# A linear-attention and mixture-of-experts kernel: a query's feature maps meet the state in two row tiles of 64 features by 128 tokens, where they met in four quarters of 64 by 64

## The chip, the cores and the metric

The kernel runs on one core of a Trainium2 chip. The metric is the device time in microseconds (us) of one execution; the median of a few runs is given, and one further execution is taken by the profiler. Nearly everything is computed in 32-bit floats; many operands are split into a high and a low part, so that three matmuls of reduced precision (fp32r) stand for one exact product. The matmuls that the change touches are plain fp32 ones.

## The reference

Two mixers of the same 2048 tokens of 448 features are weighted by a gate per token. A is linear attention with 16 heads of 28 features and a learned feature map, B a mixture of 8 experts of which each token uses two.

```python
q, k, v = heads(x @ wqkv)                                   # 16 heads, Dh = 28
phi = lambda p: concat([softmax(p @ w_phi), softmax(-(p @ w_phi))])   # 56 features a head
kv  = einsum("bhsf,bhsd->bhfd", phi(k), v)                  # the state, summed over tokens
z   = einsum("bhsf->bhf", phi(k))
num = einsum("bhqf,bhfd->bhqd", phi(q), kv)
den = einsum("bhqf,bhf->bhq", phi(q), z) + 1e-6
a   = (num / den) @ wo
b   = sum over the token's two experts e of gate_e * (silu(x @ w1[e]) @ w2[e])
g   = sigmoid(sum(x * gate_w))
out = g * a + (1 - g) * b
```

The change is in `num` and `den`: the maps of the queries times the state.

## The kernel before

The kernel has three stages on the time axis. Up to about 113 us it makes the keys' maps and sums the state over 16 row tiles of 128 tokens (`key`, `norm`, `state`, and `value` for the values), and folds weights together (`fold`, line 308, whose small fp32 matmuls `wf` are the same kind of quarters as those of the change). From 113 to about 204 us the queries' maps meet the state, again one row tile of 128 tokens after the other. After that the experts run, two matmul layers each (`hp` at lines 139 and 1038, `acc` at lines 1122, 1138 and 1156), to the end at 791 us.

In the middle stage, the pass of the loop for row tile t puts these on TensorE, in this order:

- `attend(t)` (line 909), the block `n`: exponentials of the query tile, turned so that features are on partitions (`et`), against the block-diagonal state `B`. A head has 64 partitions: 56 features and a pad of zeros. `et[t]` has eight columns of blocks (`NJ = 8`), and in each the partitions 0 to 63 are one head and 64 to 127 another, so all 16 heads are covered. `B` holds 28 + 28 + 4 = 60 columns for a head: the state for the positive and for the negative softmax, and the sums for the denominators.
- `flip(t + 2)` (line 729), the block `et`: 16 transposes that turn the maps of a later tile, in two row tiles of the array (64 rows by 128 columns each).
- `turn(t - 1)` (line 948), the block `ot`: eight transposes of the previous tile's result, in the same two row tiles.
- `project(t - 2)` (line 139), the block `ao`: eleven matmuls of 128 by 128 with the output weights.
- `ask(t + 7)` (line 658), the block `pq`: eleven matmuls of 128 by 128 that make the query projection of a later tile; in the later passes its place is taken by transposes of tokens for the first expert (`xgt`).

VectorE then reads `n` in `weigh` (reciprocals `r` and `n`, products `z` and `w`, lines 919 to 925), and GpSimd sums the two signs (`om`). There is one PSUM tile for `n`, two banks wide (`two_banks`, tag "T", one buffer), so `n` of the next row tile waits until VectorE has read this one. The first index of its view, `a`, picks the bank and the half of the partitions of `et`; `b` picks the half of the tokens.

The order on TensorE, ACT and VectorE is the order of the program in this part (a manual schedule). SyncE issues transfers in an order that the scheduler chooses from modelled times; its queue holds the stores of finished rows (`aos`, line 960), the loads of small tables (`byrank`, `tabm`, `tabx`) and the loads of the experts' weights (`wr`, line 772).

A shape such as 64*64 in the profile is the part of the array that an instruction uses, rows by columns. A plain fp32 matmul is two records, one for each pass, and each has a weight load of its own (LDWEIGHTS, on the row PEld), whose columns are the stationary operand's: here the tokens.

Of the kernel before, what the change touches and what calls it, by code (L numbers as in the profile page):

```python
# [84 lines left out]
def gated_mix(ctx: ExitStack, tc: tile.TileContext, xt, xq, wk, wq, wv, wphi, wo, w12, out):  # L85
    nc = tc.nc
# [18 lines left out]
    def two_banks(name, tag="T"):  # L105
        pool, n = banks[tag]
        return pool.tile([P, NJ, P], F32, tag=tag, name=name, bufs=n)
# [26 lines left out]
    reached = {}  # L134
# [77 lines left out]
    start = ExitStack()  # L212
# [28 lines left out]
    for what in LANDING:  # L241
        t = int(what[1])
# [57 lines left out]
    half = [slice(64 * a, 64 * a + 64) for a in range(2)]  # L300
# [65 lines left out]
    for what in LANDING:  # L366
        t = int(what[1])
# [297 lines left out]
    B = px.tile([P, NJ, 60], F32, name="B")  # L665
    nc.gpsimd.tensor_copy(B[:, :, 58:60], hsign.unsqueeze(1).to_broadcast([P, NJ, 2]))

    def blocks(kvs):
        nc.scalar.activation(kvs[:, :, 0:56], kvp[:, 0:224].rearrange("p (g f) -> p g f", g=4), AF.Copy)
        yield  # L670
        kvt = bank("O", "kvt")
        for g in range(0, 4, 2):
            nc.tensor.transpose(kvt[:, g * 64:g * 64 + P], kvs[:, g:g + 2].rearrange("p g f -> p (g f)"), ident)
        kv = kvt[:, 0:256].rearrange("p (j d) -> p j d", j=NJ)[:, :, 0:DH + 1]
        nc.scalar.activation(B[:, :, 0:DH + 1], kv, AF.Copy, scale=hsign[:, 0:1])
        nc.vector.tensor_scalar(B[:, :, DH + 1:58], kv, hsign[:, 1:2], None, op0=ALU.mult)
# [43 lines left out]
    et = {}  # L720
# [33 lines left out]
    b = blocks(kvs)  # L754
# [149 lines left out]
    def attend(t):  # L904
        n_ = two_banks(f"n{t}").rearrange("p (a j) (b d) -> p a (j b) d", a=2, b=2)
        for j in range(NJ):
            for a, h in enumerate(half):
                for b in half:
                    reached["n"] = nc.tensor.matmul(n_[b, a, j, 0:60], et[t][h, j, b], B[h, j], start=True, stop=True)  # L909
        return n_.rearrange("p a j d -> p (a j) d")  # L910

    def weigh(t, n_):
# [301 lines left out]
    for t in range(NT + 2):  # L1214
# [15 lines left out]
        if t < NT:  # L1230
            n_ = attend(t)
# [76 lines left out]
    for s in range(E * NFC):  # L1308
# [15 lines left out]
        if e < LARGE:  # L1324
# [5 lines left out]
            while len(held) > (1 if e == 0 or fc == 0 else 2):  # L1330
                h = held.pop(0)
# [5 lines left out]
        n = 3 * nm  # L1337
        if e == E - 1 and fc > NFC - LATE:
            n = n // 2 if fc < NFC - 1 else 0
# [121 lines left out]
```

## Time and profile before

| | |
|---|---|
| median of 3 runs | 787.98 us (787.19 to 788.23) |
| the profiled execution, its own time | 793.1 us |
| its span, first to last instruction | 791.1 us |
| mean granted TensorE clock | 0.993 |
| TensorE busy (PE), weight loads (PEld) | 776.4 us, 717.7 us |
| VectorE, ScalarE, GpSimd busy | 481.0, 308.6, 335.3 us |
| block n, line 909 | 1024 records of a load, 1024 of a matmul, 113.6 to 199.6 us |

Matmuls are pipelined: a record of a matmul lasts from its issue to a modelled end, and records overlap, so the sum of busy time says less than the distance from the start of one block to that of the next. Weight loads overlap matmuls. "issue" as a releaser means that the engine waited for nothing that the profile shows. Times in the profile count from the start of the span.

### The profile page before, as it was taken

The numbers are of one execution on the slowest core, as the hardware profiler recorded it, in microseconds if no ns is written. First come the engines' busy times: TensorE is split into PE (matmuls) and PEld (weight loads), VectorE is DVE, ScalarE is ACT, GpSimd is POOL, SyncE is SP. The second block draws the span as 40 slices with busy tenths as digits, with TensorE's granted clock in tenths as the row PEclk, the third lists the DMA queues.
The fourth block names the chain that finished last, engine by engine and source line by source line (L and its number), as shares of the span: only waits on it lengthen the run. The fifth ranks groups of instructions, "written<-read, shape, count | busy, mean of one in ns | idle before, by whom it ended". The sixth has DMA issues, their size and how long they took to land.

```text
span 791.1 us, 18474 instructions
## 1 busy us (share of the span) xinstructions
PE 776.4 (98%) x7542; PEld 717.7 (91%) x7542; DVE 481.0 (61%) x1044; ACT 308.6 (39%) x523; POOL 335.3 (42%) x318
## 2 busy tenths in 40 slices
PE   8999999999999999999999998999999999999995
PEld 6888878888999999998998898999999999999994
DVE  4698977768776865665574443554744555475431
ACT  5543455556532443343342322332433333243221
POOL 5667877885123235414540445144325405523003
PEclk9999999999999999999999998999999999999998
DMA  8320000153333346326541552363445436434403
GB/s 274 125 86 1 2 2 26 27 119 138 121 140 127 105 90 180 99 81 148 157 131 53 116 149 91 107 153 128 123 119 151 135 118 161 137 129 109 138 2 47
DMA packets 39788, 85.95 MB, mean 109 GB/s; under 512 B 11312, under 2 KB 20928, under 8 KB 39700
## 3 DMA queue, kind: packets, MB, share of 16 engines
q1 hardware_dynamic: 29332, 67.88, 25.9%
q0 software_dynamic: 10224, 16.61, 11.3%
q8 instruction: 61, 1.00, 0.6%
q10 hardware_dynamic: 144, 0.23, 0.1%
q14 instruction: 27, 0.22, 0.1%
HBM read 71.89 MB, written 12.82 MB: 107 GB/s over the span
## 4 chain that ended last, share of the span: by engine, by line
PE 86%; issue 9%; DVE 1%; POOL 1%; ACT 1%; DMA 0%; SPq 0%; POOLq 0%; DVEq 0%; ACTq 0%
PE hp L1038 17%; PE acc L1122 17%; PE hp L139 15%; PE acc L1156 13%; PE ao L139 5%; PE pk L139 5%; PE pq L658 3%; PE pv L139 3%; PE n L909 2%; PE pv L353 1%; PE early L658 1%; PE kv L637 1%; PE et L729 1%; POOL out_dram L994 1%; PE acc L1138 1%
## 5 line engine op out<-in xcount | busy, mean ns | idle before, releaser
L1122 PE MATMUL acc<-w2h,hx 64*128 64x448 f32 (+3 forms) x1088 | 193.5, 365 | 0.1
L1071 ACT ACTIVATE hs<-hp 128x272 f32<-128x272 f32 (+4 forms) x154 | 70.8, 484 | 312.2 <-issue 190.0
L828 POOL DMA_INDIRECT xg<-in_xq_dram,idq x114 | 125.5, 1101 | 156.6 <-PE hp L1038 56.5
L1077 DVE CAST hx<-hs 128x504 fp32r<-128x504 f32 (+5 forms) x154 | 55.4, 360 | 209.9 <-ACT hs L1071 203.9
L1122 PEld LDWEIGHTS acc<-w2h,hx 64*128 64x128 f32 (+3 forms) x1088 | 159.6, 184 | 5.9 <-ACT y L1179 1.5
L1122 PE MATMUL acc<-w2l,hx 64*128 64x448 f32 (+3 forms) x544 | 153.8, 365 | 0.0
L1038 PE MATMUL hp<-xgl,w1h 64*128 64x504 f32 (+2 forms) x490 | 144.6, 386 | 1.9 <-issue 1.9
L1038 PE MATMUL hp<-xgh,w1h 64*128 64x504 f32 (+2 forms) x490 | 145.0, 386 | 0.6 <-issue 0.6
L1038 PE MATMUL hp<-xgh,w1l 64*128 64x504 f32 (+2 forms) x490 | 144.4, 387 | 0.1
L994 POOL DMA_INDIRECT out_dram<-y,tabm x32 | 52.2, 1632 | 172.4 <-DVE y L1181 164.0
L1156 PE MATMUL acc<-w2h,hx 128*128 128x448 f32 (+2 forms) x366 | 111.7, 365 | 0.0
L1122 PEld LDWEIGHTS acc<-w2l,hx 64*128 64x128 f32 (+3 forms) x544 | 95.7, 184 | 1.6
L1038 PEld LDWEIGHTS hp<-xgl,w1h 64*128 64x128 f32 x490 | 86.2, 185 | 4.6 <-issue 1.8
L1038 PEld LDWEIGHTS hp<-xgh,w1h 64*128 64x128 f32 x490 | 86.3, 185 | 4.2 <-issue 1.3
L1038 PEld LDWEIGHTS hp<-xgh,w1l 64*128 64x128 f32 x490 | 85.9, 185 | 4.0 <-issue 0.9
L1080 DVE TENSOR_TENSOR hx<-hs,hx 128x276 fp32r<-128x276 f32 (+5 forms) x168 | 84.9, 512 | 5.3
L139 PE MATMUL hp<-xgh,w1h 128*128 128x272 f32 (+1 forms) x336 | 87.9, 289 | 0.0
L139 PE MATMUL hp<-xgh,w1l 128*128 128x272 f32 (+1 forms) x336 | 87.8, 289 | 0.0
L797 DVE TENSOR_TENSOR w1l<-wr,w1h 128x1024 fp32r<-128x1024 f32 x56 | 68.2, 1218 | 10.9 <-ACT w1h L795 10.0
L1156 PEld LDWEIGHTS acc<-w2h,hx 128*128 128x128 f32 (+2 forms) x366 | 68.0, 186 | 6.2 <-issue 0.7
L1156 PE MATMUL acc<-w2l,hx 128*128 128x448 f32 (+2 forms) x190 | 69.4, 365 | 0.0
L139 PEld LDWEIGHTS hp<-xgh,w1l 128*128 128x128 f32 x336 | 63.2, 188 | 0.6
(235 smaller groups left out, 1396.1 us busy)
## 6 DMA issues: line engine op xcount, KB each, us to landing
wr<-in_w_dram SPq DMA_DIRECT2D x56, 512.0 KB
wr<-in_w_dram SPq DMA_DIRECT2D x46, 448.0 KB
kept<-in_w_dram SPq DMA_DIRECT2D x10, 448.0 KB
out_dram<-aos SPq DMA_DIRECT2D x16, 224.0 KB
xr<-in_xt_dram SPq DMA_DIRECT2D x10, 256.0 KB
xg<-in_xq_dram,idq POOLq DMA_INDIRECT x114
xr<-in_xt_dram SPq DMA_DIRECT2D x6, 192.0 KB
out_dram<-zero SPq DMA_DIRECT2D x5, 224.0 KB
```

The lines of the kernel that those rows point to most:

```text
L139: reached["pe"] = nc.tensor.matmul(o, a, b, start=i == 0, stop=i == n - 1)
L658: nc.tensor.matmul(pq[t].rearrange("p h d -> p (h d)"), x, w, start=k == 0, stop=k == 10)
L797: nc.vector.tensor_tensor(out=l, in0=raws[s][layer - 1], in1=h.bitcast(F32), op=ALU.subtract)
L828: i = nc.gpsimd.indirect_dma_start(out=t[:, b], out_offset=None, in_=xq, in_offset=bass.IndirectOffsetOnAxis(ap=idq[:, e, 4 * c + b:4 * c ...
L909: reached["n"] = nc.tensor.matmul(n_[b, a, j, 0:60], et[t][h, j, b], B[h, j], start=True, stop=True)
L994: return nc.gpsimd.indirect_dma_start(out=out, out_offset=bass.IndirectOffsetOnAxis(ap=idx_ap, axis=0), in_=y, in_offset=None, compute_op= ...
L1038: meet(("first", i), a, lambda: nc.tensor.matmul(o[i], l, r, start=n == 0, stop=n == len(rounds) - 1), n == 0)
L1071: nc.scalar.activation(hs[:, tsl], hp, AF.Silu)
L1077: nc.vector.tensor_copy(h[:, tsl], hs[:, tsl])
L1080: nc.vector.tensor_tensor(out=h[:, a + o:b + o], in0=hs[:, a:b], in1=h[:, a:b].bitcast(F32), op=ALU.subtract)
L1122: meet((e, c), a, lambda: nc.tensor.matmul(acc[e][c][:l.shape[1], 0:D], l[half[a]], r[half[a]], start=new, stop=ends and c not in of[k + 1 ...
L1156: i = nc.tensor.matmul(acc[e][c][:l.shape[1], 0:D], l, r, start=fc == 0 and k == 0, stop=fc == NFC - 1 and k == len(pr) - 1)
```

## The change

The loop over the two halves of the tokens goes; the stationary operand is now all 128 tokens of the tile (64 rows by 128 columns) instead of 64 of them (64 by 64), and the result covers all 128 partitions of its bank instead of half of them. The moving operand stays the 60 columns of `B`. So a row tile has 16 matmuls instead of 32, on two row tiles of the array instead of four quarters. What is computed is the same, and lands in the same places.

```diff
         n_ = two_banks(f"n{t}").rearrange("p (a j) (b d) -> p a (j b) d", a=2, b=2)
         for j in range(NJ):
             for a, h in enumerate(half):
-                for b in half:
-                    reached["n"] = nc.tensor.matmul(n_[b, a, j, 0:60], et[t][h, j, b], B[h, j], start=True, stop=True)
+                reached["n"] = nc.tensor.matmul(n_[:, a, j, 0:60], et[t][h, j], B[h, j], start=True, stop=True)
         return n_.rearrange("p a j d -> p (a j) d")
```

On TensorE's queue, in the pass for the third row tile, the rows before (a name, its number, then the partitions and columns that are written):

```order
L658 MATMUL pq_1827<-WHq,XL_178 128x448 x3
L909 MATMUL n_1854<-B,et_1693 64x60 [waits DVE_49,PE_49]
L909 MATMUL n_1854<-B,et_1693 64x60 x31
L729 MATMUL et_1903<-ident,eq_210 128x64 [waits Activation_49,Pool_49]
L729 MATMUL et_1904<-ident,eq_210 128x64 [waits Activation_49]
```

and now:

```order
L658 MATMUL pq_1795<-WHq,XL_178 128x448 x3
L908 MATMUL n_1822<-B,et_1677 128x60 [waits DVE_49,PE_49]
L908 MATMUL n_1822<-B,et_1677 128x60 x15
L729 MATMUL et_1855<-ident,eq_210 128x64 [waits Activation_49,Pool_49]
L729 MATMUL et_1856<-ident,eq_210 128x64 [waits Activation_49]
```

Nothing moved on TensorE: 32 rows became 16, of twice the partitions, with the same waits, between the same neighbours. The queues of VectorE, ScalarE and GpSimd hold the same instructions in the same order.

On SyncE's queue, at the end of the small tables and the start of the experts' weights, the rows before:

```order
L971 DMA tabm<-tabd 128x4x2
L960 DMA out_dram<-aos_2632 128x448
L772 ISA
L772 DMA wr_0_2777<-in_w_dram 128x1024
L772 ISA
L772 DMA wr_0_2778<-in_w_dram 128x896
```

and now:

```order
L970 DMA tabm<-tabd 128x4x2
L772 ISA
L772 DMA wr_0_2633<-in_w_dram 128x1024
L959 DMA out_dram<-aos_2504 128x448
L772 ISA
L772 DMA wr_0_2634<-in_w_dram 128x896
```

The sixth store of a finished row moved behind the first load of weights. The fourth and the fifth moved in the same way, behind five and one more loads of `byrank`; the other stores stand where they stood.

## The prediction

> **What bounds the kernel now.** I read the page first (busy shares, then the chain that ended last), then the chain in order of time around the changed line, then the busy time by stage, and last the weight loads kept apart by shape.
>
> ```profile
> PE 776.4 (98%) x7542; PEld 717.7 (91%) x7542; DVE 481.0 (61%) x1044; ACT 308.6 (39%) x523; POOL 335.3 (42%) x318
> PE 86%; issue 9%; DVE 1%; POOL 1%; ACT 1%; DMA 0%; SPq 0%; POOLq 0%; DVEq 0%; ACTq 0%
> 113.60:204.00 90.40, 89.00 (x1650) 78.88 (x1650) 68.87 (x167) 55.02 (x98) 63.15 (x59) 1.00 0.26 73
> 204.00:791.00 587.00, 576.17 (x4662) 544.45 (x4660) 324.56 (x695) 198.97 (x314) 194.64 (x157) 0.99 0.42 119
> ```
>
> TensorE is busy 98% of the span and makes up 86% of the chain. The two rows by stretch give its busy time first, then weight loads, DVE, ACT, POOL, the granted clock and the DMA share. In the stage of the change (113.6 to 204 us) it works 89.00 of 90.40 us at full clock, so what is put on it or taken from it there moves the end, but for 1.4 us. After 204 us it is again the engine that everything waits for. The chain in one ordinary row tile of this stage (start, length, what):
>
> ```profile
> 137.06 1.09 PE n L909 x64
> 138.15 0.64 PE et L729 x16
> 138.79 0.25 PE ot L948 x8
> 139.04 2.43 PE ao L139 x11
> 141.47 2.22 PE pq L658 x11
> 143.70 1.09 PE n L909 x64
> ```
>
> Nothing but TensorE stands between one tile's n and the next, 6.64 us later: no wait of 0.1 us is in it. The changed block is 1.09 us of it. It has 64 records for 32 matmuls: fp32 goes in two passes, each with its own weight load.
>
> **What sets those 1.09 us.** The change makes half as many matmuls of twice the width, so all depends on whether a pass costs its issue, its streaming, or its weight load. First the same block as loads (PEld) and matmuls (PE), with two blocks of other code for comparison (start, length from first to last, count):
>
> ```profile
> 143.62 1.02 PEld L909 LDWEIGHTS n<-B,et 64*64 64x64 f32 x64 [0.30 <-issue]
> 144.71 0.57 PEld L729 LDWEIGHTS et<-ident,eq 64*128 64x128 f32 x16
> 145.21 0.33 PEld L948 LDWEIGHTS ot<-ident,om 64*128 64x128 f32 x8
> 143.63 1.16 PE L909 MATMUL n<-B,et 64*64 64x60 f32 x64
> 19.60 1.97 PEld L308 LDWEIGHTS wfk<-bd,wraw_k 64*64 64x64 f32 x128 [0.31 <-issue]
> 48.32 0.45 PEld L637 LDWEIGHTS kv<-ek,v 128*32 128x32 f32 x32
> ```
>
> and the mean length of one load, by shape (the number before the bar's idle part is busy us, then ns of one):
>
> ```profile
> L637 PEld LDWEIGHTS kv<-ek,v 128*32 128x32 f32 x512 | 7.2, 109 | 4.5 <-issue 3.7 <-POOL ek L628 0.3 <-POOL XH L152 0.3
> L909 PEld LDWEIGHTS n<-B,et 64*64 64x64 f32 x1024 | 16.9, 134 | 5.5 <-issue 5.0 <-DVE B L676 0.4
> L308 PEld LDWEIGHTS wfk<-bd,wraw_k 64*64 64x64 f32 x128 | 2.0, 135 | 0.3 <-issue 0.3
> L1156 PEld LDWEIGHTS acc<-w2h,hx 128*80 128x80 f32 x14 | 2.1, 148 | 0.0
> L1122 PEld LDWEIGHTS acc<-w2h,hx 64*120 64x120 f32 x168 | 30.3, 180 | 0.4
> L1038 PEld LDWEIGHTS hp<-xgh,w1h 64*128 64x128 f32 x490 | 86.3, 185 | 4.2 <-issue 1.3 <-ACT hs L1071 0.3
> L729 PEld LDWEIGHTS et<-ident,eq 64*128 64x128 f32 x224 | 8.0, 138 | 0.9
> L467 PEld LDWEIGHTS <-ones_b 128*128 128x128 bf16 x16 | 0.6, 97 | 0.0
> ```
>
> Four tiles of the array work at once in n, wfk and kv, two in et. A round is one load and one pass on each tile, and its length is (block minus one load) / (rounds minus 1):
> - n: (1020 - 134) / 15 = 59 ns, moving 60 columns, loading 64.
> - wfk (64*64 too): (1970 - 135) / 31 = 59 ns, moving 56, loading 64.
> - kv: (450 - 109) / 7 = 49 ns, moving 56 as wfk does, loading 32.
> - et (transposes): (570 - 138) / 7 = 62 ns, loading 128.
>
> wfk and n have the same round although they move 56 and 60 columns; kv, which moves 56, is faster with half the load. So n is held by its load, not by streaming. Nor is it held by issue: kv puts out a pass every 49/4 = 12 ns, n every 15.
>
> The load's length grows with the number of columns, with the number of rows without effect: 109, 134, 148, 180, 185 ns for 32, 64, 80, 120, 128 columns of matmul weights. Only transposes (138 at 128 columns) and bf16 (97) are off this line. The new load is a matmul's, 64 rows by 128 columns of 32-bit data: the row at the same shape is L1038's, 185 ns. I take it; it is 51 ns above today's 134.
>
> **The change, part by part** (a tile is a row tile of 128 tokens; there are 16).
> - Removed: 16 of 32 matmuls a tile, so 32 of 64 loads and passes. They are worth nothing by themselves: the four quarters ran side by side in 16 rounds, the two row tiles will run side by side in 16 rounds as well.
> - Longer rounds: 59 + 51 = 110 ns, over 15 intervals 15 x 51 = 765 ns, and the last load is itself 51 ns longer: +0.82 us to the end of the block.
> - The change of shape between n and et goes: both become 64*128. Now et's first load starts 70 ns after the last load of n has ended (143.62 + 1.02 = 144.64, then 144.71). Between et and ot, both 64*128, the next load starts 70 ns before the last has ended (144.71 + 0.57 = 145.28, ot at 145.21). So -0.14 us where et follows.
> - What is ahead of n (pq, ao, xgt at 128*128) differs from it in shape as before: 0.
>
> A tile with et behind it: 0.82 - 0.14 = +0.68 us. In the last two tiles n is followed by ao at 128*128, as here:
>
> ```profile
> 194.31 1.16 PE L909 MATMUL n<-B,et 64*64 64x60 f32 x64
> 195.40 0.47 PE L139 MATMUL ao<-WHo,oh 128*128 128x448 f32 x1
> ```
>
> There the shape still changes: +0.82 us each. The first tile is the one whose successor waits for VectorE, which is busy with something else when n(0) ends:
>
> ```profile
> 113.63 1.16 PE L909 MATMUL n<-B,et 64*64 64x60 f32 x64
> 114.26 1.03 DVE mxq L597
> 115.29 0.27 DVE r L919
> 117.74 0.14 issue
> 117.88 1.16 PE n L909 x64
> ```
>
> n(0) ends at 113.63 + 1.16 = 114.79, r starts at 115.29. With 0.82 us more it ends at 115.61 and r starts at about 115.7: +0.4 us for that tile, the rest falls into the wait.
>
> - SyncE's queue issues three stores of finished rows (aos) a little later: the fourth behind five more loads of byrank, the fifth behind one, the sixth behind one load of weights (wr). Only the last of them has transfers of size ahead of it:
>
> ```profile
> 172.19 1.35 SPq L960 DMA_DIRECT2D out_dram<-aos  x1
> 174.22 1.74 SPq L772 DMA_DIRECT2D wr<-in_w_dram  x4
> 179.52 0.65 ACT L959 ACTIVATE aos<-ao,gt 128x448 f32<-128x448 f32 x1
> ```
>
> The sixth store goes out 2 us later, at about 174.2. aos has three buffers, so it holds up only the ninth row's copy on ACT, which starts at 179.52 in any case: 5 us of cover, 0. Were that cover gone, ACT would keep a bank that the next ao needs, by as much as the store is late.
>
> No new wait is added. What reads n (r, z, w on VectorE, then om on GpSimd) starts later by as much as TensorE does, and the time from n's end to the next n, in which w must be done, keeps its et, ot, ao and pq.
>
> Sum: 13 x 0.68 + 2 x 0.82 + 0.4 = 8.84 + 1.64 + 0.4 = 10.9 us. It is made against the profiled execution, 793.1 us (a span of 791.1 and 2.0 around it): 804.0. The median of the runs, 787.98, is 5.1 us below that execution; I put the same 10.9 us on it, since nothing in the sum depends on what differs: **798.9 us**, 1.4% slower.
>
> Bounds on the terms. If the drain between n and et were kept, 13 x 0.14 = 1.8 us more: 800.7. If all idle time of TensorE in the stage covered some of it, 1.4 us less: 797.5. TensorE also has a few stalls that no other engine ends, such as these (the middle row: 2.5 us in three waits of L1038, the longest 0.9), and half as many instructions in n may move or end one: 1 us either way. So 796.5 to 801.7 for this case.
>
> ```profile
> 130.94 0.58 PE L909 MATMUL n<-B,et 64*64 64x60 f32 x21 [0.40 <-issue]
> PE hp L1038 <- issue: 2.5, 3, 0.9
> 485.04 0.47 PE L1038 MATMUL hp<-xgl,w1h 64*128 64x504 f32 x1 [0.94 <-issue]
> ```
>
> **Rivals.**
> 1. The wide load is as quick as et's, 138 ns at the same 64*128. Then a round is 62 or 63 ns: 15 x 4 = +0.06, less 0.14, so -0.08 x 13 + 0.06 x 2 = -0.9 us: 787.1, no change that can be told. For it: it is the nearest row by shape, data and place. Against it: et is a transpose, and each of the matmul loads, 64*128 among them, lies on the other line.
> 2. On the other side, faster: the wide load becomes a fast one as the bf16 load is, 97 ns for 128 columns. Then streaming binds, 49 x 60/56 = 52 ns a round: 15 x -7 = -0.1, the tail -0.04, the drain -0.14, so -0.28 x 13 - 0.14 x 2 = -3.9 us: 784.1. It decides as soon as a load is below some 127 ns. Against it: 490 loads of 128 columns of 32-bit data at 185. [...]
> 3. Issue binds after all, so that half the passes take half the time, 32 x 17 = 0.54 us: -0.54 - 0.14 = -0.68 x 13 - 0.54 x 2 = -9.9 us: 778. Against it: kv's 12 ns a pass. [...]
> 4. The loads of the two row tiles don't overlap: 32 x 110 - 16 x 59 = +2.6 us a tile, some 39 us in all: 827. Against it: et's 16 loads on two row tiles take 0.57 us, and one behind another 16 x 62 would be 0.99.
> 5. More of it is covered than the 1.4 us, the 2.5 us of stalls of L1038 falling away as well: 10.9 - 3.9 = +7: 795.
>
> **How the numbers follow.** The forecast 0.80; rival 5 0.07, rival 1 0.05, rival 2 0.03, rival 4 0.03, rival 3 0.02. The range takes the likeliest case's own, 796.5 to 801.7, and rival 5: 795 to 802. A difference of 0.2%, 1.6 us, is about what a measurement of this kernel can tell from none. Slower: 0.80 + 0.07 + 0.03 = 0.90; same: 0.05; faster: 0.03 + 0.02 = 0.05.
>
> **What would show it.** In the profile after, n has 512 loads and passes of 64*128; the mean load is about 185 ns (at 138 rival 1, near 97 rival 2 holds); the block of 32 loads takes about 1.84 us from first to last, against 1.02; et's first load starts before n's last has ended; the next n comes 7.3 us after the one before in the ordinary tiles, against 6.64; r of the first tile starts near 115.7. TensorE's busy time in L909's group cannot be used for this, since overlapping passes hide in it. I am wrong if the round is near 59 ns with a load of 185, which would mean that a load can be two passes ahead.

## The result, and the profile after

The median is 798.37 us (797.29 to 798.93) against 788.11 us (787.19 to 788.35) for the kernel before, run beside it: a ratio of 1.0131 (95% interval 1.0113 to 1.0148), 10.3 us slower. The forecast was 798.9 us in a range of 795 to 802. The profiled execution took 798.15 us, with a span of 796.1 us.

The page, engine totals and the shares of the chain that ended last:

```profile
PE 784.7 (99%) x7030; PEld 732.9 (92%) x7030; DVE 486.0 (61%) x1044; ACT 310.1 (39%) x523; POOL 336.1 (42%) x318
PE 87%; issue 8%; DVE 2%; POOL 1%; ACT 1%; DMA 0%; POOLq 0%; DVEq 0%; ACTq 0%
```

TensorE has 512 fewer records (7030 for 7542) and is busy 8.3 us longer. Half the instructions took more time. The chain in an ordinary row tile (start, length, what), to be held against the six rows of before:

```profile
132.14 1.93 PE n L908 x32
134.07 0.51 PE et L729 x16
134.57 0.25 PE ot L947 x8
134.82 2.43 PE ao L139 x11
137.25 2.23 PE pq L658 x11
139.48 1.95 PE n L908 x32
```

`n` has gone from 1.09 to 1.93 us, `et` from 0.64 to 0.51, and the other three stand as they were: 7.34 us from one `n` to the next where it was 6.64. So +0.70 us a tile. The block as weight loads, then the mean of one load by shape (busy us, then ns of one):

```profile
146.74 1.86 PEld L908 LDWEIGHTS n<-B,et 64*128 64x128 f32 x32 [0.30 <-issue]
148.47 0.64 PEld L729 LDWEIGHTS et<-ident,eq 64*128 64x128 f32 x16
```
```profile
L1037 PEld LDWEIGHTS hp<-xgh,w1l 64*128 64x128 f32 x490 | 87.3, 185 | 1.9
L908 PEld LDWEIGHTS n<-B,et 64*128 64x128 f32 x512 | 29.9, 188 | 4.4 <-issue 3.4 <-PE pp L467 0.6 <-DVE B L676 0.4
L729 PEld LDWEIGHTS et<-ident,eq 64*128 64x128 f32 x224 | 9.0, 146 | 0.0
```

The wide load of `n` took 188 ns, beside 185 for the row from which its price was taken and 146 (138 before) for the transposes of the same shape. A round, by the same formula as in the prediction, is (1860 - 188) / 15 = 111 ns where it was 59. And `et`'s first load starts at 148.47, ahead of the end of `n`'s last at 148.60, where before it started 70 ns behind it.

The stage as a whole: it runs from the first `n` (113.63 before) to the `ao` behind the last `n`. First the chain after, then the chain before (its stall in the fourth tile, and its end):

```profile
114.84 2.02 PE n L908 x32
...
116.89 0.37 DVE r L918
...
119.58 1.99 PE n L908 x32
...
204.27 1.93 PE n L908 x32
...
209.38 1.87 PE n L908 x32
211.25 0.81 PE ao L139 x3
```
```profile
129.39 1.14 PE n L909 x43
130.53 0.40 issue
130.94 0.58 PE n L909 x21
...
194.38 1.09 PE n L909 x64
...
198.71 1.09 PE n L909 x64
199.80 1.84 PE ao L139 x8
```

Before it is 199.80 - 113.63 = 86.17 us, after 211.25 - 114.84 = 96.41: +10.24 us, beside the medians' +10.26 (that they agree to 0.02 is chance, since the interval of the ratio alone is 8.9 to 11.7 us). Nothing outside the stage is needed to explain them. The two profiled executions differ by 5.1 us only. With the change the stage starts 1.2 us later, which isn't the change's doing: in the experiments below it starts at 114.87 with quarters (120 moving columns) and at 113.64 with the change run again. And before holds a stretch among the experts, 6.4 us longer between the same instructions, that the other lacks; behind it the two agree to 0.15 us. 10.24 + 1.21 - 6.4 = 5.05. The busy time by stretch (TensorE first, the granted clock third from the end), before and after:

```profile
478.00:490.00 12.00, 9.39 (x67) 8.29 (x65) 7.07 (x16) 4.12 (x6) 7.88 (x9) 0.83 0.41 128
```
```profile
488.00:500.00 12.00, 12.00 (x115) 12.00 (x113) 7.01 (x16) 4.13 (x6) 9.25 (x10) 1.00 0.42 135
```

That is where before's waits of L1038 lie that the prediction quoted.

### The profile page after: what moved, and what is told of

Read it like the earlier page. It is cut to its first block, busy times and chain, and to the rows that moved or that the text cites. A ratio compares the mean times of both kernels' runs of the same rounds, so it can differ in the third digit from the quotient of the medians.

```text
span 796.1 us, 17450 instructions
## 1 busy us (share of the span) xinstructions
PE 784.7 (99%) x7030; PEld 732.9 (92%) x7030; DVE 486.0 (61%) x1044; ACT 310.1 (39%) x523; POOL 336.1 (42%) x318
## 3 DMA queue, kind: packets, MB, share of 16 engines
q0 software_dynamic: 10224, 16.61, 11.2%
## 4 chain that ended last, share of the span: by engine, by line
PE 87%; issue 8%; DVE 2%; POOL 1%; ACT 1%; DMA 0%; POOLq 0%; DVEq 0%; ACTq 0%
PE acc L1121 17%; PE hp L1037 16%; PE hp L139 15%; PE acc L1155 13%; PE pk L139 5%; PE ao L139 5%; PE n L908 4%; PE pv L139 3%; PE pq L658 3%; PE pv L353 2%; PE early L658 1%; PE kv L637 1%; POOL out_dram L993 1%; PE acc L1137 1%; PE et L729 1%
```

## A wait that is new

One tile in the stage is 0.8 us longer than the others: in the chain the `n` of 139.48 and the one at 154.97 are two tiles apart, 15.49 us, and with 7.34 for the first of them the second takes 8.15. TensorE waits for VectorE there, and VectorE sits in one small operation (L514). VectorE and GpSimd after, then the same in the kernel before (L514 and L516 took 0.22 us each):

```profile
144.99 3.57 DVE L514 TENSOR_TENSOR more<-er,upto 128x64 f32<-128x64 f32 x1
148.59 0.23 DVE L516 TENSOR_TENSOR more<-more,upto 128x64 f32<-128x64 f32 x1
```
```profile
145.65 1.16 POOL L929 TENSOR_TENSOR om<-w 128x448 f32<-128x448 f32 x1
146.76 1.71 POOL L602 TENSOR_TENSOR eq<-eq,mxq 128x896 f32<-128x896 f32 x1
```
```profile
PE ot L947 <- DVE ol L153: 0.6, 1, 0.6
```
```profile
141.76 0.22 DVE L514 TENSOR_TENSOR more<-er,upto 128x64 f32<-128x64 f32 x1
142.02 0.22 DVE L516 TENSOR_TENSOR more<-more,upto 128x64 f32<-128x64 f32 x1
```
```profile
143.19 1.16 POOL L930 TENSOR_TENSOR om<-w 128x448 f32<-128x448 f32 x1
```

`er` and `upto` are both in SBUF. L514 ends 0.09 us after GpSimd's `eq` does (148.56 and 148.47). In the kernel before, L516 had ended 0.95 us ahead of `om`; after the change L514 started 0.66 us ahead of it. Behind L514 stand `oh` and `ol` of the same tile, so `ot` of the next pass on TensorE is late by 0.6 us. By the records L514 started first and waited all the same (GpSimd's records are rough): 3.57 us against 0.22. That it waits for GpSimd is read from these times; by what mechanism, the trace doesn't show. The experiments' traces have the same pattern: in seven of them too an L514 or L516 that started 0.17 to 0.67 us ahead of this `om` ended some 0.09 us after `eq`, with quarters in the array as well as with the wide shape. So the meeting is a matter of when the two engines come, and not of the shape of `n`.

## The experiments

They ran on three chips, on each of which the kernel before has a median of 794.3 or 794.4 us (788.1 beside the change above), so ratios are compared. My theory: a round is held by the weight load of each row tile, which lengthens with its columns. The rivals: streaming, the issue of an instruction, or a cost set off once, early in the stage.

**The change again, on one of these chips.** Unchanged code.

> The change itself, on the chip of the experiments. By the first comparison it is 1.31% slower than before, 10.4 us here. If the chip mattered to it, the ratio would be outside 1.011 to 1.015.

804.32 us, ratio 1.0134 (1.0113 to 1.0155). The ratio is the same here within the error; the experiments are read against this run, +9.9 us.

**Twice the moving columns in the change.**

```diff
-                reached["n"] = nc.tensor.matmul(n_[:, a, j, 0:60], et[t][h, j], B[h, j], start=True, stop=True)
+                js = slice(j, min(j + 2, NJ))
+                reached["n"] = nc.tensor.matmul(n_[:, a, js, 0:60], et[t][h, j], B[h, js], start=True, stop=True)
```

Here 14 of the 16 matmuls of a tile stream 120 columns, and the later pass overwrites what the earlier one left.

> The changed kernel, but each matmul of n streams 120 columns of the state instead of 60 (the columns of the next block too; what they write is overwritten by the matmul of that block, so the result is the same). Theory (a round is held by the weight load of 128 columns, 112 ns measured): 120 columns stream in some 2 x 52 = 104 ns, which is still below 112, so the block stays at 1.83 us and the kernel at 798.4 us, within 1.5 us. Rival (the round grew because a pass through 128 columns of the array streams or writes slower): 14 of 16 rounds double, +1.6 us a tile, some 823 us.

804.57 us, ratio 1.0121 (1.0098 to 1.0144), as the change. The block as loads:

```profile
146.62 1.86 PEld L909 LDWEIGHTS n<-B,et 64*128 64x128 f32 x32 [0.30 <-issue]
```

The same 1.86 us to the digit: streaming twice as much is hidden altogether under the loads. Streaming doesn't hold the changed block. VectorE's wait shows here as well, in the next operation: L514 started 0.73 us ahead of `om` and took 0.23, and L516, 0.47 ahead, took the wait.

```profile
145.13 3.37 DVE L516 TENSOR_TENSOR more<-more,upto 128x64 f32<-128x64 f32 x1
```

**Twice the moving columns in the kernel before.** The same edit on quarters.

> The kernel before (quarters of 64 by 64), each matmul of n streaming 120 columns instead of 60 in the same way. Theory: the round is the longer of load (59 ns) and streaming (about 104 ns, up to 110 if the 6 ns between a pass and the next load come on top): 14 x 45 to 51 ns = +0.63 to +0.71 us a tile, 797.5 to 799 us, about what the change costs. Rival (the round has nothing to do with streaming at all): 788 us, unchanged.

802.42 us, ratio 1.0116 (1.0091 to 1.0141).

```profile
146.48 1.64 PEld L910 LDWEIGHTS n<-B,et 64*64 64x64 f32 x64 [0.30 <-issue]
```
```profile
L910 PEld LDWEIGHTS n<-B,et 64*64 64x64 f32 x1024 | 26.5, 133 | 4.4 <-issue 3.6 <-DVE B L676 0.4 <-remote 0.3
```

With loads of the same 133 ns the round rises from 59 to (1640 - 133) / 15 = 100 ns on average; by the single loads in the trace the first is 54 ns and the others, with 120 columns, are 102 to 103. So streaming is worth up to 103 / 120 = 0.86 ns a column, some 51 ns for 60, and in the kernel before it lay just under the load. As the run before this one shows, a round is the longer of the two, not their sum.

**Tokens in 32s.** Half the load's columns once more, eight tiles of the array, 64 matmuls a row tile.

```diff
-                for b in half:
+                for b in range(0, P, 32):
+                    b = slice(b, b + 32)
```

> The kernel before, cut the other way: eight tiles of 64 rows by 32 tokens, 64 matmuls a row tile instead of 32. Theory (load by columns): a load of 32 columns is 109 ns instead of 134, so streaming holds the round, 52 ns against 59 (or still 56 to 59 if 6 ns come on top in row tiles), and the first load is 26 ns shorter: -0.05 to -0.16 us a tile, 785.5 to 787.5 us. Rival (the number of instructions counts, 12 ns a pass): 128 passes in 1.5 us, +0.45 us a tile, 795 us.

814.22 us, ratio 1.0232 (1.0206 to 1.0258): both were too low, my theory by far.

```profile
137.30 1.30 PEld L910 LDWEIGHTS n<-B,et 64*32 64x32 f32 x128 [0.30 <-issue]
```
```profile
L910 PEld LDWEIGHTS n<-B,et 64*32 64x32 f32 x2048 | 21.5, 106 | 14.0 <-issue 13.3 <-DVE B L676 0.4 <-remote 0.3
```
```profile
119.60:125.00 5.40, 1.94 (x130) 1.64 (x132) 1.23 (x2) 1.93 (x3) 2.79 (x2) 0.81 0.03 3
125.00:130.00 5.00, 5.00 (x34) 4.52 (x35) 4.50 (x10) 1.57 (x3) 2.31 (x2) 0.52 0.01 3
```
```profile
PE n L910 <- issue: 9.3, 6, 3.4
```

The load is short as expected (106 ns), but 128 passes take 1.30 us at best, 10 ns each: by all signs the issue binds at last, as the rival had it with 12. The single records fit this: in this block the first 33 loads start some 6 ns apart on average, the later ones mostly in pairs 17 ns apart, with no pause after every eight, where the kernel before starts four loads 6 to 7 ns apart and then pauses for 39 ns. And six times TensorE stood still at or within `n` with nothing that the trace shows to wait for, 9.3 us in all, the longest 3.4 us; after that one the granted clock fell (0.52 from 125 to 130 us). With more instructions of less work the supply of instructions seems to run dry; that is inferred from the missing releaser, not shown. By these runs quarters lie between two limits: the load for wider tiles, the issue for narrower ones.

**One row tile after the other.** The loops over `j` and `a` in the change are exchanged, so that the 16 passes of the upper half of the rows come first.

```diff
-        for j in range(NJ):
-            for a, h in enumerate(half):
+        for a, h in enumerate(half):
+            for j in range(NJ):
```

> The changed kernel with the two loops of n exchanged: all eight matmuls of the upper row tile, then all eight of the lower. Theory (loads of the two row tiles overlap only because the program alternates between them, and passes start in program order): 32 loads one behind another, 32 x 112 = 3.6 us a block, +1.8 us a tile, some 825 us. Rival (the array works ahead on the other row tile whatever the order): 798.4 us, unchanged.

836.93 us, ratio 1.0525 (1.0506 to 1.0545).

```profile
153.59 2.91 PEld L908 LDWEIGHTS n<-B,et 64*128 64x128 f32 x29 [0.30 <-issue]
```
```profile
113.60:208.00 94.40, 94.38 (x720) 86.33 (x719) 46.14 (x101) 37.20 (x64) 47.43 (x44) 0.80 0.17 48
```

29 of the 32 loads need 2.91 us, where all of them took 1.86; by the single records, loads of one row tile start 111 to 112 ns apart. So each row tile has a chain of loads of its own, and the two chains run side by side only while the instructions alternate. This is the prediction's rival 4, brought about on purpose: it isn't what the change does. The rest of the 42.6 us comes with a granted clock of 0.80 in the stage, 1.00 in the change.

**Half of the row tiles wide**, once the later half, once the earlier one.

```diff
-                for b in half:
+                for b in ([slice(0, P)] if t >= 8 else half):
```

(and `t < 8`)

> Row tiles 8 to 15 have the change, 0 to 7 have quarters. My theory (the price lies in the block n itself and is paid tile by tile): six tiles with et behind at +0.70 us, the last two at +0.78 us each, 5.8 us slower than before; ordinary tiles 6.63 us apart up to the eighth and 7.33 us from the ninth. Rival (most of the price comes once, from a stall or a collision that the change sets off early in the stage, as VectorE's wait in the sixth tile): 1 to 3 us slower.

> The other half: row tiles 0 to 7 have the change. My theory: 0.48 for the first tile and 7 x 0.70 for the others, 5.4 us, less up to 1.5 us of the stall of TensorE in the fourth tile of the kernel before, plus 0.8 us if VectorE's wait in the sixth tile comes as it did with the change: 4 to 6 us slower than before. This run and the one with the wide tiles from the ninth on then add up to the change's +10.3 us within the error. Rival (something in the early tiles, such as the stall that goes, decides the size): they don't add up, by more than 2 us.

799.19 us and 1.0075 (1.0055 to 1.0096) for the later half, 799.88 us and 1.0066 (1.0047 to 1.0085) for the earlier: +6.0 and +5.2 us by the ratios (+4.9 and +5.6 by the medians), together 11.2 (10.5) where the change has 10.4 (1.0131 of 794.3) to 10.6 (1.0134), inside the error. The chain of the first of the two where the shape changes:

```profile
158.34 1.09 PE n L909 x64
...
164.97 1.93 PE n L909 x32
...
172.31 1.93 PE n L909 x32
```

6.63 us up to the first wide tile, 7.34 from it on. The price is paid tile by tile. Where the early tiles are quarters, the stall of 0.4 us in the fourth tile is there as in the kernel before; where they are wide, it is gone, and L514 takes 3.59 us as with the change.

**Two of the eight column blocks in quarters.**

```diff
-                for b in half:
+                for b in ([slice(0, P)] if j not in (2, 5) else half):
```

> As the change, but the third and the sixth of the eight column blocks stay in quarters, so the shape changes four times inside n. Four rounds fall from 112 to 59 ns: -212 ns a tile. My theory: a change between 64*128 and 64*64 costs the 90 ns by which the step from n to et is longer than a round before (149 against 59), so 4 x 90 = +360, in sum +0.15 us a tile, 2.4 us slower than the change (12.7 slower than before). Rival 1 (a change of shape costs nothing, and the 149 ns are only et's first load): -0.21 us a tile, 3.4 us quicker than the change (7 slower than before). Rival 2 (a change of shape waits until the array is empty, a load and a pass, some 190 ns): 4 x 190 - 212 = +0.55 us a tile, 9 us slower than the change.

812.02 us, ratio 1.0217 (1.0199 to 1.0234): 17.2 us above before by the ratio, 6.6 to 6.8 above the change, between my theory (2.4) and rival 2 (9). An ordinary tile in the chain:

```profile
142.72 2.31 PE n L909 x40
```

`n` is 2.31 us, 0.38 more than in the change, and four short rounds had given back 4 x 53 = 0.21. So four changes of shape cost 0.59 us, 148 ns each. My 90 ns had counted the step from `n` to `et` alone (149 against 59, where the like step within `n` is 39) and left out that the first round behind it is longer too; the prediction's 0.14, read from the loads, was the right figure. Over 16 tiles the 0.38 make 6.1 of the 6.6 to 6.8 us.

**One pass instead of two.** `et` and `B` are rounded to fp32r, so the second pass and its precision are left out.

```diff
-    B = px.tile([P, NJ, 60], F32, name="B")
+    B = px.tile([P, NJ, 60], F32R, name="B")
...
-        et[t] = pt.tile([P, NJ, P], F32, tag="et", name=f"et{t}", bufs=2)
+        et[t] = pt.tile([P, NJ, P], F32R, tag="et", name=f"et{t}", bufs=2)
```

> As the change, but et and B are rounded to the reduced type (fp32r), so a matmul is one pass with one load where it was two; the second pass and its precision are left out. My theory (the block is a chain of loads of 188 ns, a round of 112): 8 rounds where there were 16, 7 x 112 + 150 = 0.93 us a block where it was 1.83, 0.90 us x 16 = 14 us quicker than the change, 4 us quicker than before. Rival (the round is held by the streaming of wide passes, and a single pass of the reduced type with only 60 columns streams as long as two): the block stays near 1.83 us, and the time at the change's.

793.25 us, ratio 0.9986 (0.9976 to 0.9996): 1.1 us quicker than before, about 11 quicker than the change.

```profile
144.15 0.97 PEld L908 LDWEIGHTS n<-B,et 64*128 64x128 f32 x16 [0.30 <-issue]
```

The block did what the theory says: half the loads at the same (970 - 188) / 7 = 112 ns a round. The 4 us that I expected against before were too many. In the chain, a tile holds

```profile
137.72 1.01 PE n L908 x16
138.72 0.55 PE et L729 x16
139.27 0.29 PE ot L947 x8
```

where I expected 0.93 for `n`, and the change has 0.51 and 0.25 for the other two: 0.08 us a tile are given back in `n` and as much behind it, some 1.1 us each over 14 tiles; why is open. And TensorE now waits for others ahead of `ot`, 0.4 us each for `ol` and `om` and 0.5 in two waits for `xgh`. It is the only version that beat the kernel before, by almost nothing and with less precision.

**The ranks step one pass later.** In the change, L514 and L516 are moved behind one more `yield`, away from `om`.

```diff
         nc.vector.tensor_reduce(out=er, in_=c1, axis=AX.X, op=ALU.add)
+        yield
```

> As the change, but the comparison and the product of the ranks step (VectorE, er against upto) come one pass of the loop later, so that they no longer run just ahead of GpSimd's om in the sixth tile. My theory (a VectorE operation with two operands in SBUF that starts shortly ahead of om and eq waits until both have ended): the 3.57 us of that operation fall to 0.22 us, the wait of ot for ol (0.6 us) goes, and the seventh n starts about 7.33 us after the sixth where it was 8.15: 0.8 us quicker than the change run beside it. Rival (the operation is slow for another reason, or another one waits in its place): it takes 3 us in its new place as well, or ot waits as before; no difference to the change.

803.42 us, ratio 1.0113 (1.0096 to 1.0130), 0.9 us below the change run beside it. By the times alone that isn't told apart from nothing; the trace tells it (the operation is L515 here):

```profile
152.11 0.22 DVE L515 TENSOR_TENSOR more<-er,upto 128x64 f32<-128x64 f32 x1
```
```profile
147.76 1.93 PE n L909 x32
...
155.09 0.92 PE n L909 x13
```

0.22 us for 3.57, and 7.33 us to the next `n` where there were 8.15. But VectorE still waits: another operation has taken the place, as the second half of the rival had it, though `ot` doesn't wait as before.

```profile
152.88 3.50 DVE L521 CAST byrank<-of 128x8 int32<-128x8 f32 x1
```

This copy of eight numbers took 0.20 us in the kernel before. Now it starts 0.63 us ahead of `om` and ends with `eq`. TensorE pays little for it: `oh` and `ol` are done just before `ot` needs them, and the next tile takes 7.46 us in place of 7.34. So the collision, not the operation, was slow, and the delay moved the collision to where it costs 0.1 us in place of 0.8; it didn't end it. L521 reads one operand, so such a wait doesn't need two operands in SBUF.

## Why the prediction was right, step by step

- *The load prices the block, and the wide load is L1038's 185 ns*: it is 188, doubling the streaming leaves the block as it was, and halving the number of passes didn't shorten it. What no run separates is the load from some fixed part of a pass on a wide tile, since each pass here has a load of its own; for the load speaks that its record grows with the columns as the round does (next point).
- *Rounds of 59 + 51 = 110 ns, +0.82 us to the block's end*: 111 to 112 ns, and the chain has +0.84. The prediction took the 51 ns from the difference of two records of loads. The three shapes of `n` say what such a record is: 106, 134 and 188 ns for 32, 64 and 128 columns are about 0.85 ns a column and 79 ns on top. By the rounds (59 and 112 ns, 53 / 64 = 0.83 ns a column and 6 on top) only the first part holds the next load back; the rest overlaps, which is why a load of 188 ns fits a round of 112.
- *-0.14 us where `et` follows in the same shape*: `et` is 0.13 us shorter in the chain, and a change of shape costs 148 ns by an experiment of its own.
- *First tile +0.4 us, the rest falling into VectorE's wait*: `n(0)` to `r` is 116.89 - 114.84 = 2.05 us, 1.66 before, +0.39. The next `n` comes 4.74 us after the first, 4.25 before: +0.49. The time of 115.7 for `r` was off only because the whole stage started 1.2 us later in this execution.
- *Last two tiles +0.82 each*: +0.78 each (5.11 us between them for 4.33, and 1.87 for 1.09 in the last).
- *Three stores moved, nothing*: TensorE's two waits for other engines in the stage name `ol` and `pos`, none a store.
- *No new wait is added*: wrong. VectorE's wait for GpSimd reaches TensorE with 0.6 us ahead of `ot`, and the tile is 0.8 us longer. The prediction saw that what reads `n` starts later, but not what VectorE would meet there.
- *Stalls, 1 us either way*: one went. The fourth tile's `n` took 2.23 us before, with 0.10 of wait ahead of it and 0.40 within, 1.14 more than an ordinary one, and is regular now.

The sum as measured: 13 x 0.70 + 0.49 + 1.56 + 0.8 = 11.95; the stage grew by 10.24; of the 1.7 between them 1.14 is the fourth tile's stall, and the other 0.6 are three longer pieces of the chain before: `ot` in the third tile with a wait ahead of it (0.28), and `ot` and `n` near the end (0.13 and 0.15). So the predicted 10.9 was right in its main terms, those of the load. The rest is a stall that went, of the kind that the prediction had allowed 1 us for, and a wait that came, which it had ruled out; that the two nearly cancelled is luck.

No rival holds: the load isn't 138 or 97 ns, fewer instructions gave nothing, and the loads do overlap. Nor does rival 5, in which the stalls of L1038 fall away: they differ from one execution to the next. The change's profile above is without them (TensorE is busy for all of the 20.00 us from 480 to 500, where before has 17.39); in the one of the change run again, with a mean granted clock of 0.992 for 0.997, it is busy for 17.29 of them.

## What to carry to other kernels

Where small fp32 matmuls share the array, price a round as the longer of the load on one tile of the array (here 0.83 ns for each column of the stationary operand, plus 6) and the streaming (here at most 0.86 ns for each moving column), and check the sum against the issue (10 ns a pass in the block of 128, by the one run that reached it). Fewer and wider matmuls gained nothing here (16 for 32 in a tile, +0.70 us), since the tiles of the array that they gave up had been loading side by side. Count each change of tile shape between neighbouring blocks (148 ns here) and keep the row tiles alternating in the program's order (32 loads took 1.86 us so, 29 took 2.91 with one row tile after the other).

## What the runs showed that I had not expected

- With the row tiles one after the other, TensorE is busy 94.38 of 94.40 us, yet its granted clock is 0.80. In the change it is busy 93.20 us of the same stretch, at 1.00. So the share of busy time didn't tell the clock here; what set it, the runs don't show.
- With 128 short passes in a block TensorE stands still now and then (9.3 us in six waits without a releaser). The kernel before has one such wait of 0.4 us in the stage, at 64 passes a block; the profile of the change above has none at 32.
- A VectorE operation of 0.22 us became one of 3.57 when the work ahead of it came to lie 0.8 us later against GpSimd's (0.66 us ahead of `om`, 1.43 before), and where it was moved away another one took the wait. A change on one engine can set off such a meeting between two others, worth 0.8 us of TensorE here, or 0.1 where the meeting has cover.
